# Storing ready-made quarters of the second-level factors from SBUF later, group by group, in a Strassen-Winograd attention-MoE kernel

## The chip, the cores and the metric

The kernel runs on one core of a Trainium2 chip. The metric is the device time of one execution in microseconds (us). A core has engines that run side by side, each with its own queue of instructions: PE (matrix products; its weight loads are listed as PEld), DVE (elementwise), ACT (activations and copies), POOL and SP. In this kernel POOL and SP do little but issue transfers (DMA) between the DRAM of the chip and SBUF, the memory on the core. An instruction waits for others by semaphores, and whatever stands behind it on its queue waits too. Results of PE land in banks of PSUM, which DVE or ACT must read before PE writes them again.

## The reference

A linear attention with decay, block by block, feeds a layer with a hidden size of 2048:

```python
for b in range(nb):                       # blocks of 64 positions
    intra = einsum('bhic,bhjc->bhij', qb, kb) * Dmask
    intra = einsum('bhij,bhjd->bhid', intra, vb)
    inter = einsum('bhid,bhde->bhie', qb * lam_pow, kv_state)
    out[:, :, sl] = intra + inter
    kv_state = lam_block * kv_state + einsum('bhsd,bhse->bhde', kb * rev_pow, vb)
x = out.transpose(0, 2, 1, 3).reshape(B * S, H * D)   # (3072, 512)
h = x @ w_in                                          # (512, 2048)
g = h - np.tanh(h)
return g @ w_out                                      # (2048, 512)
```

The inputs are q, k, v of shape (4, 8, 768, 64), float32; lam of shape (8,); w_in and w_out.

## The kernel before, in words

The 3072 tokens are done in six groups of 512 (128 positions of each of four batches), numbered 0 to 5. A group is: attention, the input product x @ w_in, the nonlinearity, the output product g @ w_out. The loop over groups is staggered: while PE does the output product of one group, the attention and input product of the next are woven in (`attention`, `inner_steps`, `in_turn`), in an order written out by hand.

Both large products are done by Strassen-Winograd, with 7 products of half size in place of 8; from the second group on some of the seven are split once more in the same way. That second level covers products 5 and 6 of the output product from group 1, 4 from group 2, 7 and 3 from group 3 (`twice`). The weight side of such a product needs sums of weight blocks, here called factors:

- `factors`, in DRAM, holds the seven first-level factors of w_out, each 128 rows by 8 blocks (kt) by 256. `sums_out(kt)` (L263) makes one block with four subtractions on DVE and stores it by three transfers on POOL's queue (L272 to L274).
- `fine`, in DRAM, holds the second-level factors: for each of the five products in `TWICE` = (3, 5, 6, 4, 7) seven pieces x of 256 KB, in the order `SUB`. Of a first-level factor cut in quarters b11, b12, b21, b22, three pieces are quarters as they are (x = 1, 2, 3 are b11, b21, b22), and four are sums (x = 5, 7, 6, 4).

The three plain quarters are stored in the first group: `sums_out` has behind its own stores a loop that copies for even kt the first, for odd kt the second and third kind of quarter of all five products into `fine`, in two transfers each (L278 with 64 KB, L279 with 256 KB, in rows of 512 bytes). Over the eight blocks these are 24 transfers and 3.93 MB, issued between 76.6 and 138.3 us.

The four sums are made later, product by product in the order `MADE` = (5, 6, 4, 7, 3). `load_quarters(t)` (L759) loads the four quarters of the t-th of these from `factors` into SBUF by four POOL transfers of 256 KB (L769). `factors_twice(t)` (L772) makes four subtractions on DVE (L781), in the order x = 5, 7, 6, 4, and stores each at once (L782). For t = 0 and 1 the four results go to tiles of their own. For t = 2, 3, 4 they are written in place, into the loaded quarters, which lie in a free part of the hidden tokens' tile (shown as gS): x = 5 goes over b11, 7 over b12, 6 over b22, 4 over b21. The loads of t = 0 and 1 come just ahead of group 1's loop and their sums within it (`make_factors`); the loads of t = 2 come late in group 1 and those of t = 3 late in group 2; their sums stand among the steps of `in_turn`, which also holds the loads and the sums of t = 4, in group 2.

POOL's queue also carries the stream of weight pieces: `piece` keeps eight tiles `wb` of 256 KB filled ahead of PE, from `fine_in` (L792), `fine` (L795) or `factors` (L798); a load waits until PE has read the tile's last content. Also on POOL: stores of results (L815) and, in group 0, raw weights (L216), which SP loads too. SP loads q, k and v: `load_natural` (L138; k_nat, v_nat) and `load_blocks` (L151; 16 transfers for each q_blk and k_blk).

Near the sums of t = 3 stand on DVE L864 and L866, which add product 7 of group 2 (PSUM tile `plain`, in bank z) into two results; `inner_steps` has the matmuls of the next group's input product (L697), some of which write into that bank afterwards. Raw weights are rounded in `round_block` (ACT L291 and following, DVE L296); transposes of q_blk and k_blk are L335, decays of k_nat L404 on ACT, the nonlinearity L600 (ACT) and L601 (DVE).

Of the kernel before, what the change touches and what calls it, by code (L numbers as in the profile page):

```python
# [24 lines left out]
def kernel(  # L25
# [32 lines left out]
    nc = tc.nc  # L58
# [66 lines left out]
    def tied(yes, op):  # L125
        return tc.keep_in_program_order(op) if yes else op
# [67 lines left out]
    SUB = (1, 2, 6, 5, 7, 3, 4)  # L194
    GI = 2
    TWICE = (3, 5, 6, 4, 7)
    fine = dram.tile([len(TWICE), len(SUB), 128, NU, 128], F32, name="fine")
# [65 lines left out]
    def sums_out(kt):  # L263
        bt, tt = pair[kt]
        b11, b12, b21, b22 = (bt[:, x] for x in range(4))
        t1, t2, t4, t3 = (tt[:, x] for x in range(4))
        nc.vector.tensor_tensor(t1, b12, b11, op=AL.subtract)
        nc.vector.tensor_tensor(t2, b22, t1, op=AL.subtract)
        nc.vector.tensor_tensor(t3, b22, b12, op=AL.subtract)
        nc.vector.tensor_tensor(t4, b21, t2, op=AL.subtract)  # L270
        f = factors[:].rearrange("x p k c -> p x k c")
        nc.gpsimd.dma_start(out=f[:, 0:1, kt, :], in_=bt[:, 0:1, :])  # L272
        nc.gpsimd.dma_start(out=f[:, 1:3, kt, :], in_=bt[:, 2:4, :])
        nc.gpsimd.dma_start(out=f[:, 3:NX, kt, :], in_=tt[:, 0:4, :])  # L274

        for x, j in ((1, 0),) if kt % 2 == 0 else ((2, 0), (3, 1)):
            dst = fine[:, SUB.index(x), :, kt // 2, :].rearrange("n p c -> p n c")
            nc.gpsimd.dma_start(out=dst[:, 0:1], in_=bt[:, 3:4, ts(j, 128)])  # L278
            nc.gpsimd.dma_start(out=dst[:, 1:5], in_=tt[:, 0:4, ts(j, 128)])  # L279

    def round_block(w, raw64, first):

# [470 lines left out]
    MADE = (5, 6, 4, 7, 3)  # L753
    quarters = {}
# [4 lines left out]
    def load_quarters(t):  # L759

        for i in range(2):
            for j in range(2):
                if t == 0:
                    x = late["pool"].tile([128, NU, 128], F32, name="wq", tag="wb", bufs=RING)
                elif t > 1:
                    x = hidden(GI + (t > 2), "S1")[:, 2 * i + j].rearrange("p m (v c) -> p (m v) c", v=2)
                else:
                    x = opool.tile([128, NU, 128], F32, name="oq", tag="o")
                tied(t > 1, nc.gpsimd.dma_start(out=x, in_=quarter_source(t, i, j)))  # L769
                quarters[t, i, j] = x  # L770

    def factors_twice(t):  # L772

        b11, b12, b21, b22 = (quarters.pop((t, i, j)) for i in range(2) for j in range(2))
        if t > 1:
            t1, t3, t4, t2 = b11, b12, b21, b22
        else:
            t1, t2, t3, t4 = (late["pool"].tile([128, NU, 128], F32, name=f"wt{x}", tag="sums", bufs=4)
                              for x in (1, 2, 3, 4))
        for x, dst, a, b in ((5, t1, b12, b11), (7, t3, b22, b12), (6, t2, b22, t1), (4, t4, b21, t2)):  # L780
            tc.keep_in_program_order(nc.vector.tensor_tensor(dst, a, b, op=AL.subtract))  # L781
            nc.gpsimd.dma_start(out=fine[TWICE.index(MADE[t]), SUB.index(x)], in_=dst)  # L782
            yield
# [324 lines left out]
    def make_factors(step):  # L1108
        t = TURNS.get(step)
        if t is not None:  # L1110
            if t not in making:
                making[t] = factors_twice(t)
            next(making[t])

# [4 lines left out]
    for g in range(1, NG):  # L1119
        last = g == NG - 1  # L1120
        (p0, p1), step = ahead, 0
        for u in range(NU):
            if u == 0:
                load(g * B + B + 1 if g + 1 < NG else 0)
                kd = decays(g + 1, (0, 1))
            if g < GI:
                for n in (2, 6, 5, 7, 1, 4, 3):
                    if n != 1:
                        up(g, u, n)
                    elif u + 1 < NU:  # L1130
                        up(g, u + 1, 1)
                    else:
                        every(down(g, 1))
                    if u == 0 and n == 5:
                        sums_in(3)
                    step += 1
                    make_factors(step)
                    some(kd, u > 0)
                inner_weights(u, (2, 4, 1))
                if u == 2:  # L1140
                    every(kd)
                if u > 1:
                    run(p0[u - 2:2 * u - 3])
                continue
            if u == 0:
                first = down(g, 1)
                next(first)
                seeded(g, 0, 6)
            if u + 1 < NU:
                seeded(g, u + 1, 6)  # L1150
            for n in (7, 1, 3) if u == 0 else (7, 3, 1) if u + 1 < NU else (7, 3):
                if n == 1:
                    next(first)
                else:
                    seeded(g, u, n)
                some(kd, 2)
            seeded_sums(g, u)
        if g >= GI:
            run(p0[1:3])
        if twice(g, 4):  # L1160
            sums_twice(g, 4)
        every(down(g, 2))
        run(p0[3:4])
        sums_twice(g, 5)
        zw = ("w", "z") if g >= GI else ("z", "w")
        p4 = down_twice(g, 4, zw[0]) if twice(g, 4) else down(g, 4)
        next(p4)
        run(p0[4:])
        every(p4)
        if g < GI:  # L1170
            run(p1[0:1])
        every(kd)
        kd = decays(g + 1, (2, 3))
        if g < GI:
            for u in (0, 1):
                inner_weights(u, (5,))
        sums_once(g, 21, 21, 11)
        sums_twice(g, 6)
        for i, _ in enumerate(down_twice(g, 5, zw[1])):
            some(kd, 2)  # L1180
            if g >= GI and i == 1:
                run(p1[0:1])
        every(kd)
        run(p1[1:3])
        if g < GI:
            for u in (2, 3):
                inner_weights(u, (5,))
            load_quarters(2)
        if twice(g, 7):
            sums_twice(g, 7)  # L1190
        every(down_twice(g, 6, zw[0]))
        if twice(g, 3):
            sums_twice(g, 3)
        run(p1[3:4])
        p7 = down_twice(g, 7, zw[1]) if twice(g, 7) else down(g, 7)
        next(p7)
        run(p1[4:])
        if g == GI:
            load_quarters(3)
        if g < GI:  # L1200
            for u in (0, 1):
                inner_weights(u, (6,))
        every(p7)
        if last:
            down_end(g)
            continue
        if g < GI:
            for u in (2, 3):
                inner_weights(u, (6,))
        ahead = attention(g + 2) if g + 2 < NG else ([], [])  # L1210
        early_pieces = [(att_transpose, g + 2, (0,)), (att_transpose, g + 2, (1,))] if g + 2 < NG else []
        inner_tokens(g + 1, (1,))
        p3 = down_twice(g, 3, "w") if twice(g, 3) else down(g, 3)
        parts = {"down": p3}
        for kind, x in in_turn(g):
            if (kind, x) == (5, 1):
                inner_tokens(g + 1, (5, 2))
                every(parts[1])
                every(p3)
            if (kind, x) == (4, 1):  # L1220
                inner_tokens(g + 1, (4, 6))
                every(parts[5])
                every(parts[2])
                if g >= GI:
                    run(early_pieces)
            if kind not in parts:
                parts[kind] = inner_steps(g + 1, kind)
            next(parts[kind])
            if kind == 1 and x in ((6, 3) if g >= GI else (3,)):
                run(early_pieces[:1])  # L1230
                early_pieces = early_pieces[1:]
            if g < GI and (kind, x) == (4, 5):
                every(factors_twice(2))
            if g == GI and (kind, x) == (1, 5):
                every(factors_twice(3))
            if g == GI and (kind, x) == (5, 6):
                load_quarters(4)
            if g == GI and (kind, x) == (6, 7):
                every(factors_twice(4))
            if kind == 6 and x in (5, 6, 2, 7):  # L1240
                seeded(g + 1, (5, 6, 2, 7).index(x), 11)
                if g < GI and x == 6:
                    run(early_pieces)
        for p in parts.values():
            every(p)
# [30 lines left out]
```

## Time and profile before

| | us |
|---|---|
| median of three runs | 649.3 (646.28, 649.30, 653.39) |
| the profiled execution | 649.38 |
| its span | 647.6 |
| PE busy in the span | 635.9 |
| DVE busy | 477.6 |
| ACT busy | 267.3 |
| POOL busy | 228.6 |
| landing of a wb load from fine, median | 4.0 |
| landing of a quarter (gS from factors), median | 7.5 |

The profile is of one execution. Its parts are: busy time of each engine; the span in 40 equal slices, each digit the busy share in tenths; DMA queues; the chain of work that ended last; groups of instructions by line; DMA issues with the time from issue to landing. In a timeline a row has the start, the duration, the engine, the line, what is written from what, the count, and in brackets how long the engine was idle before it and what released it. The granted clock of PE is at full speed in all slices.

### The profile page before, as it was taken

How to read it: one execution, taken by the hardware profiler on the slowest of the kernel's cores; microseconds unless marked ns; L12 is line 12 of the kernel's file. 1: busy time of each engine (PE TensorE's matmuls, PEld its weight loads, DVE VectorE, ACT ScalarE, POOL GpSimd, SP SyncE). 2: the span in 40 equal slices, each digit the busy share in tenths (PEclk: the TensorE clock that was granted, in tenths of full speed). 3: DMA queues.
4: the chain of work that ended last, by engine and by line, in shares of the span. 5: the costliest groups of instructions: out<-in, count | busy, mean ns of one | idle time of the engine just before them, and what ended most of it. 6: DMA issues, size and time to landing. Idle time of an engine off the chain costs nothing.

```text
span 647.6 us, 16635 instructions
## 1 busy us (share of the span) xinstructions
PE 635.9 (98%) x6440; PEld 584.0 (90%) x6440; DVE 477.6 (74%) x948; ACT 267.3 (41%) x620; POOL 228.6 (35%) x397
## 2 busy tenths in 40 slices
PE   8899999999999999999999999999999999999998
PEld 7788888888888899998999998999998899998997
DVE  4468697785898867569967569988667987467953
ACT  4789676503432422345331247333245332334310
POOL 0000255735443454410455431355321254520161
PEclk9999999999999999999999999999999999999999
DMA  9979998969765999775889986798884577832484
GB/s 215 219 192 245 315 273 278 346 191 266 207 167 124 294 264 303 210 191 121 211 242 289 289 211 160 173 280 242 261 182 96 134 237 241 246 104 76 102 287 150
DMA packets 166190, 139.80 MB, mean 216 GB/s; under 512 B 136864, under 2 KB 138016, under 8 KB 166112
## 3 DMA queue, kind: packets, MB, share of 16 engines
q0 software_dynamic: 31792, 104.62, 51.1%
q1 hardware_dynamic: 134176, 34.12, 26.2%
q8 instruction: 51, 0.84, 0.6%
q14 instruction: 27, 0.22, 0.1%
q10 hardware_dynamic: 144, 0.00, 0.0%
HBM read 111.94 MB, written 26.74 MB: 214 GB/s over the span
## 4 chain that ended last, share of the span: by engine, by line
PE 46%; issue 19%; DMA 10%; DVE 8%; POOL 8%; SPq 6%; ACT 3%; POOLq 0%; DVEq 0%; ACTq 0%
PE acc L994 7%; PE h L965 6%; DMA q_blk<-in_q_dram 5%; PE y L906 5%; SPq L151 4%; PE plain L849 4%; PE y L554 4%; POOL wb L795 4%; PE zw L906 3%; PE y L697 3%; PE z L554 2%; POOL wb L792 2%; DMA k_blk<-in_k_dram 2%; DMA k_nat<-in_k_dram 1%; PE z L697 1%
## 5 line engine op out<-in xcount | busy, mean ns | idle before, releaser
L795 POOL DMA_DIRECT2D wb<-fine x133 | 71.7, 540 | 159.2 <-PE plain L849 108.8
L849 PE MATMUL plain<-wb,g 128*128 128x256 f32 x416 | 96.0, 381 | 0.0
L849 PEld LDWEIGHTS plain<-wb,g 128*128 128x128 f32 x416 | 77.5, 190 | 10.4
L965 PE MATMUL h<-xt,w 128*128 128x256 f32 x256 | 58.3, 382 | 1.4 <-DVE w L296 1.4
L798 POOL DMA_DIRECT2D wb<-factors x64 | 34.5, 540 | 71.2 <-PE z L697 47.9
L910 ACT ACTIVATE q<-y 128x128 f32<-128x128 f32 x76 | 21.1, 278 | 87.4 <-PE y L906 86.3
L965 PEld LDWEIGHTS h<-xt,w 128*128 128x128 f32 x256 | 47.5, 190 | 8.7 <-DVE w L296 1.8
L906 PE MATMUL y<-wb,g 128*128 128x128 f32 x336 | 44.8, 278 | 0.0
L792 POOL DMA_DIRECT2D wb<-fine_in x60 | 32.5, 544 | 28.8 <-PE z L697 10.8
L600 ACT ACTIVATE th<-g 128x512 f32<-128x512 f32 x48 | 29.4, 627 | 29.8 <-DVE g L625 29.6
L906 PEld LDWEIGHTS y<-wb,g 128*128 128x128 f32 x336 | 40.7, 192 | 0.7
L688 ACT ACTIVATE g<-y 128x512 f32<-128x512 f32 x24 | 14.3, 597 | 63.1 <-PE y L697 63.1
L404 ACT ACTIVATE k_nat<-k_nat,mask 128x64 f32<-128x64 f32 (+1 forms) x128 | 35.0, 335 | 1.7 <-DMA k_nat<-in_k_dram 1.7
L994 PE MATMUL acc<-wt,g 128*128 128x256 f32 x144 | 32.9, 380 | 0.2 <-DVE g L973 0.2
L601 DVE TENSOR_TENSOR g<-g,th 128x512 f32<-128x512 f32 x48 | 32.1, 683 | 0.4
L697 PE MATMUL z<-tt,wb 128*128 128x128 f32 x256 | 31.9, 275 | 0.0
L994 PEld LDWEIGHTS acc<-wt,g 128*128 128x128 f32 x144 | 27.2, 190 | 4.3 <-DVE g L973 0.6
L906 PE MATMUL zw<-wb,g 128*128 128x128 f32 x224 | 30.2, 278 | 0.1
L619 PE MATMUL y<-xt,w 128*128 128x256 f32 x128 | 30.3, 379 | 0.0
L619 PE MATMUL zs<-xt,ws 128*128 128x256 f32 x128 | 30.2, 379 | 0.0
L697 PEld LDWEIGHTS z<-tt,wb 128*128 128x128 f32 x256 | 30.2, 192 | 0.0
L292 ACT ACTIVATE r<-raw 128x512 int16<-128x512 uint32 x32 | 25.2, 787 | 8.8 <-DMA raw<-in_moe_w_out_dram 4.6
(236 smaller groups left out, 1475.0 us busy)
## 6 DMA issues: line engine op xcount, KB each, us to landing
wb<-fine POOLq DMA_DIRECT2D x133, 256.0 KB, 4.0
wb<-factors POOLq DMA_DIRECT2D x64, 256.0 KB, 4.3
wb<-fine_in POOLq DMA_DIRECT2D x60, 256.0 KB, 4.8
v_nat<-in_v_dram SPq DMA_DIRECT2D x24, 256.0 KB, 5.2
raw<-in_moe_w_out_dram POOLq DMA_DIRECT2D x12, 512.0 KB, 6.0
k_nat<-in_k_dram SPq DMA_DIRECT2D x20, 256.0 KB, 4.9
fine<-wt POOLq DMA_DIRECT2D x17, 256.0 KB, 3.5
raw<-in_moe_w_in_dram SPq DMA_DIRECT2D x8, 512.0 KB, 5.0
```

The source lines that it names most:

```text
L404: tc.keep_in_program_order(nc.scalar.activation(k_h, k_h, AF.Copy, scale=mask[0:rows, h % 2, h // 2, HALF - 1:HALF]))
L554: nc.tensor.matmul(out=t[:, m, :], lhsT=wt[:, kt, ts(m, 128)], rhs=x[:, kt, :], start=first and m == 0 and kt == 0, stop=kt == 1, skip_gro ...
L601: nc.vector.tensor_tensor(dst(c), src, th, op=AL.subtract)
L619: nc.tensor.matmul(out=t[:, m, :], lhsT=wt[:, kt, ts(m, 128)], rhs=x[:, kt, :], start=False, stop=kt == 1, skip_group_check=True)
L697: nc.tensor.matmul(out=dst[:, ts(u, 128)], lhsT=a, rhs=b, start=(x in (1, 5) or x == 2 and not filled) and u == 0, stop=True, skip_group_c ...
L792: nc.gpsimd.dma_start(out=t.rearrange("p m c -> p (m c)"), in_=fine_in[INNER.index(n_[1]), (5, 6, 3).index(x_)].rearrange("p u c -> p (u c)"))
L795: nc.gpsimd.dma_start(out=t.rearrange("p m c -> p (m c)"), in_=fine[TWICE.index(n_), SUB.index(x_)].rearrange("p u c -> p (u c)"))
L798: nc.gpsimd.dma_start(out=t, in_=factors[XAT[FACT[n_][1]]][:, 2 * x_:2 * x_ + 2, :])
L849: tied(held["yes"], nc.tensor.matmul(out=t[:, m, :], lhsT=a[:, u, kt, ts(m, 128)], rhs=wb[:, kt, :], start=first and u == 0 and m == 0 and ...
L906: tied(held["yes"], nc.tensor.matmul(out=dst, lhsT=a[:, u, :], rhs=wb[:, ts(u, 128)], start=x in (1, 2) and u == 0, stop=u == NU - 1, skip ...
L965: tied(u == 0 or held["yes"], nc.tensor.matmul(out=hm[c][:, m, :], lhsT=w1[u][:, i, a, ts(m, 128)], rhs=xt[0, t][:, i, :], start=m == 0 an ...
L994: tied(held["yes"], nc.tensor.matmul(out=acc[n][:, r, :], lhsT=a[:, ts(r, 128)], rhs=b, start=kt == 0 and r == 0, stop=kt == KH - 1, skip_ ...
```

## The change

The loop at the end of `sums_out` goes. A new function, `quarters_alone(t)`, stores the three plain quarters of the t-th product straight from the tiles that `load_quarters(t)` has filled: three POOL transfers of 256 KB with rows of 2 KB. It is called ahead of the first sum of t = 0 and of t = 1 in `make_factors`; at the end of the output product of groups 1 and 2 for t = 2 and 3; and among the steps of group 2 for t = 4. In all 15 transfers with the same 3.93 MB. Loads and sums stay as they are. As the sums of t = 2, 3, 4 are written into the loaded quarters, the sums that overwrite b11, b22 and b21 now come after the stores of these have landed. In the changed kernel the lines behind the removed loop have numbers lower by 5, those behind the new function by 1.

```diff
@@ sums_out
         nc.gpsimd.dma_start(out=f[:, 3:NX, kt, :], in_=tt[:, 0:4, :])
-
-        for x, j in ((1, 0),) if kt % 2 == 0 else ((2, 0), (3, 1)):
-            dst = fine[:, SUB.index(x), :, kt // 2, :].rearrange("n p c -> p n c")
-            nc.gpsimd.dma_start(out=dst[:, 0:1], in_=bt[:, 3:4, ts(j, 128)])
-            nc.gpsimd.dma_start(out=dst[:, 1:5], in_=tt[:, 0:4, ts(j, 128)])
@@ behind load_quarters
+    def quarters_alone(t):
+        for x, i, j in ((1, 0, 0), (2, 1, 0), (3, 1, 1)):
+            nc.gpsimd.dma_start(out=fine[TWICE.index(MADE[t]), SUB.index(x)], in_=quarters[t, i, j])
@@ make_factors
             if t not in making:
+                quarters_alone(t)
                 making[t] = factors_twice(t)
@@ the loop over groups
         if last:
             down_end(g)
             continue
+        if g in (1, GI):
+            quarters_alone(1 + g)
         if g < GI:
@@ the steps of in_turn
+            if g == GI and (kind, x) == (4, 2):
+                quarters_alone(4)
             if g == GI and (kind, x) == (6, 7):
                 every(factors_twice(4))
```

## The prediction

> **What bounds the kernel now.** I read the page first: its engine rows and its slices.
>
> ```profile
> PE 635.9 (98%) x6440; PEld 584.0 (90%) x6440; DVE 477.6 (74%) x948; ACT 267.3 (41%) x620; POOL 228.6 (35%) x397
> PE   8899999999999999999999999999999999999998
> POOL 0000255735443454410455431355321254520161
> DMA  9979998969765999775889986798884577832484
> ```
>
> PE is busy for 635.9 of 647.6 us, so all its gaps together are 11.7 us. POOL, on whose queue the edit acts, is busy for a third of the span. The third row that matters is DMA: its engines are full (9) in many slices, also from 340 to 372 us. Then I asked for busy time by stretch, to see where the 11.7 us lie:
>
> ```profile
> 0.00:99.00 99.00, 92.31 (x1056) 79.02 (x1056) 65.61 (x137) 71.88 (x135) 15.06 (x29) 1.00 0.98 246
> 99.00:144.20 45.20, 45.20 (x217) 39.81 (x210) 34.63 (x74) 18.75 (x31) 24.87 (x39) 1.00 0.85 275
> ...
> 345.00:384.00 39.00, 39.00 (x317) 38.08 (x316) 26.92 (x54) 11.57 (x20) 19.17 (x33) 1.00 0.90 255
> ```
>
> The columns are the stretch, its length, the busy time of PE, PEld, DVE, ACT, POOL, the granted clock, the DMA share and GB/s. 6.7 us of gaps lie before 99 us, 4.0 after 552 (the tail); from 99 to 552 us only 1.0 is left. A kernel so bound by PE gains from an edit on POOL only what a PE gap holds, but loses whatever makes PE wait. Third, what the removed stores cost on POOL, from the groups by line within 75 to 144 us:
>
> ```profile
> L279 POOL DMA_DIRECT2D fine<-wt x9 | 6.8, 755 | 0.9 <-issue 0.9
> L278 POOL DMA_DIRECT2D fine<-wt x9 | 5.0, 554 | 0.0
> L279 POOL DMA_DIRECT2D fine<-ws x3 | 2.3, 754 | 0.2 <-issue 0.2
> L278 POOL DMA_DIRECT2D fine<-ws x3 | 1.7, 557 | 0.0
> ```
>
> Last, the timelines of POOL, DVE and PE around each place where stores come in. The one without room is that of MADE[3] (product 7) in the third group; three timelines in turn:
>
> ```profile
> 337.05 2.98 POOL L769 DMA_DIRECT2D gS<-factors  x4
> 341.47 0.55 POOL L798 DMA_DIRECT2D wb<-factors  x1 [1.44 <-DMA wb<-factors]
> ```
>
> ```profile
> 345.47 0.69 DVE L781 TENSOR_TENSOR gS<-gS 128x512 f32<-128x512 f32 x1 [1.34 <-DMA gS<-factors]
> ...
> 347.49 0.69 DVE L781 TENSOR_TENSOR gS<-gS 128x512 f32<-128x512 f32 x1 [1.12 <-DMA gS<-factors]
> ...
> 348.30 0.68 DVE L781 TENSOR_TENSOR gS<-gS 128x512 f32<-128x512 f32 x1
> 348.90 0.68 DVE L864 TENSOR_TENSOR q<-q,plain 128x512 f32<-128x512 f32 x1
> 349.50 0.68 DVE L866 TENSOR_TENSOR q<-q,plain 128x512 f32<-128x512 f32 x1
> ```
>
> ```profile
> 351.48 1.06 PE L697 MATMUL w<-xt,w 128*128 128x128 f32 x8
> ```
>
> DVE already waits here for the quarters' loads (1.34 and 1.12 us). Right behind the third subtraction (L781) stand L864 and L866, the last readers of PSUM bank z; in the built program the matmuls at 351.48 wait for exactly L866. It ends at 350.18, so the slack is 1.30 us.
>
> **The change part by part.** The sum is made against the profiled execution, 649.38 us (span 647.6 and 1.78 around it); that is 0.08 above the median of 649.3, so both readings are the same. Only POOL's order of instructions changes in the built program; PE, DVE, ACT and SP keep theirs.
>
> *Removed from group 0.* 12 stores of L278 by 0.55 and 12 of L279 by 0.75 us make 6.7 + 9.1 = 15.8 us of POOL's time and 3.93 MB, between 76.6 and 138.3 us. In 99–144.2 PE has no gap (45.20 of 45.20); in 75–99 it has two, 0.18 and 0.88 us, and those wait for DVE and ACT, not for a transfer. Gain: 0. L994's matmuls run there at 0.216 us each, as L554's do elsewhere, so less traffic does not make them faster. What can move is the SP queue. Its q_blk loads start at 130.63, right after the last rounding of weights (L296, 130.56). That stands behind ACT's L291, which waited 0.97 us for raw weights at 125.58 and could otherwise start only when PE's last matmul of its block ends, at 125.89. So SP starts 0 to 1 us earlier.
>
> *Added for MADE[0] and [1], 144–163.* Their 8 loads are issued 144.73–152.85; the 6 stores, 4.5 us of issue at most by the 0.75 of a load, follow as the loads land (5.4 and 6.9 us). The wb loads at 152.85–156.24 move back by some 5 us. Their first use is at 189.24, and POOL then sits idle 6.92 us until 163.16, where it waits for DVE. These factors go to tiles of their own, so no subtraction waits for a store. Cost 0; cover: 27 us of prefetch. Without that cover it would be 5 us.
>
> *Added for MADE[2], 238–244.* The 3 stores put the wb loads of 241.58 and 243.30 back by up to 2 us; PE uses them at 252.49 and 253.38, about 7 us after they land. Its subtractions (in place, like those of [3]) come at 257.50, over 8 us after the stores' issue; a store from the same tiles took 4.4 us in 248–262. Cost 0; with landings of 7.8 us the cover would just be gone.
>
> *Added for MADE[4], 366–371.* Loads 363.08–366.05, stores behind them, subtractions not before 380.82: 10 us of room. Cost 0.
>
> *Added for MADE[3], 344–352.* POOL's new order is: four loads (337.05–340.03); a store waiting for the first load; one wb; the stores waiting for the third and the fourth load; two wb. The subtractions write into the loaded tiles, so they now wait for the stores as well: the first for store 1, the third for store 3, the fourth for store 2. Store 3 cannot be issued before its quarter landed, 347.45 by DVE's own wait in the timeline. How long a store of 256 KB takes is the unknown. The same form (fine<-gS) had a median of 4.5 us in 346–364, 4.4 in 248–262 and 6.6 in 372–386; the row of L782 over the whole run goes from 2.6 to 7.4, that of the removed L279 from 2.9 to 7.8. I take 4.5, the same place: 347.5 + 4.5 = 352.0. Behind that stand the third subtraction, L864 and L866, spaced 0.60, and 0.68 for the last: 352.0 + 0.60 + 0.60 + 0.68 = 353.9. PE wants it at 351.48: **stall 2.4 us**. In short, landing time less 2.1: at 2.6 us of landing 0.5, at 7.8 it is 5.7; loads that land 1 us earlier (less SP traffic) take 1 off. The first subtraction, by store 1 (issued about 344.9, landing 349.4), is done in time for that. Behind the stall, the wb loads that the two stores put back from 342.48 and 344.08 to about 348.1 and 348.7 land at the 5.3 us of this window at about 353.4 and 354; PE wants them at 354.99 and 355.89, plus the stall: hidden, by 1.6 us if there is none. DVE then has some 3 us of arrears. Its next waits on PE are 2.19 us at 362.28 and 1.17 at 364.14, and nothing between is nearer to PE than L714 (about 1.6 us), which is late by no more than PE itself. So the stall is neither recovered nor multiplied.
>
> *Rule weighed.* Row: 4.5 us for such a store. The Trainium skill, DMA: Bandwidth & Descriptors, section Anatomy of one DMA — SWDGE (gpsimd) path, gives a transfer as about 2.0 us plus its bytes at 436 GB/s, an estimate of 2.6 us here, and hence a stall of 0.5. The trace disagrees: with DMA at 9 tenths, 4.5 was measured.
>
> Sum: 0 + 0 + 0 + 0 + 2.4 = +2.4, so 649.38 + 2.4 = **651.8 us**.
>
> **The rivals.**
> 1. *Hidden after all.* Stores land at the fast end (2.6 to 3.1 us), or PE's real slack is larger because its ends in a profile are modelled. Stall 0 to 1, time 649.4 to 650.4. For it: stores whose last bytes meet emptier queues; against: DVE's two waits for loads of 7.6 and 8.2 us in the same stretch say that the queues are full.
> 2. *Faster.* SP's stream, continuous from 130.63 to about 290, starts up to 1 us earlier. It brings k_nat at 288.90, for which ACT (L404) waited 1.73 and then DVE (L601) 3.10; from there DVE runs almost without a gap to PE's gaps of 0.59 at 304.21 and 0.10 at 319.25. If the earlier start holds, those 0.7 go: time 648.7 if the stall is hidden as well. It decides only if the stall is under 0.7. Against: between lie 0.77 MB of new stores in 232–260, where DMA is full.
> 3. *SP late.* The same chain the other way: those 0.77 MB, at the 264 to 303 GB/s moved there, are 2.8 us of a full DMA. The part that SP bears, 1 to 2.8 us, delays k_nat, and L601's chain to PE has 0 slack: 651.8 + 1 to 2.8 = 652.8 to 654.6. The Trainium skill, DMA: Bandwidth & Descriptors, section Issuing engines are not separate DMA queues, says that transfers of all queues share the same 16 engines. The trace shows that here in SP's 16 q_blk loads, which took between 7.7 and 12.8 us. Against: SP was relieved of as many bytes before.
> 4. *Slow store.* Landing of 6.6 to 7.8: stall 4.5 to 5.7, time 653.9 to 655.1.
>
> **How the numbers follow.** Stall of 1 to 4 us: 0.50 (650.4 to 653.4). Rival 1: 0.22. Rival 2: 0.08. Rival 3: 0.10. Rival 4: 0.10. The likeliest gives 651.8. The range leaves out what is beyond the ends of rivals 2 and 4 and adds about 1 us for what runs of one kernel differ (646.28 to 653.39 before): 647.5 to 656. One per cent, about what a measurement of this kernel can tell from no change, is 6.5 us. Faster by that would need over half of all PE gaps: 0.03. Slower needs a store of over 8.6 us, or rivals 3 and 4 together: 0.09. Within: 0.88.
>
> **What would show it.** In the new profile: L278 and L279 gone and PE still gapless in 99–144; a PE wait at L697 of about 2.4 us for DVE L866 near 351–354; DVE's third subtraction there (L780 in the new numbering) waiting for DMA fine<-gS until about 352; no new PE wait at 189, 252–258 and 381; PE's gaps at 304 and 319 as before within 1 us. Wrong if the wait at 351 is absent or over 4.5 us, if PE waits for wb anywhere, or if the gaps at 304 to 319 have grown.

## The result, and the profile after

The changed kernel takes 650.5 us (median of 20 runs, 648.9 to 655.73); the kernel before, run beside it, 647.51 (20 runs, 645.66 to 653.39). The ratio is 1.0044, with a 95% interval of 1.0027 to 1.0061: slower by 2.85 us (1.7 to 4.0), within 1%. A second measurement, with 12 runs, gave 1.0052 (1.0034 to 1.0071). The forecast of +2.4 us came out in sign and size, but for half the reason: there are two costs in place of one. The forecast one was smaller in most profiles than forecast, the other was not seen, and that the two errors nearly cancel is luck.

One thing must be known before the traces are laid side by side. The profiled execution after took 648.99 us, the one before 649.38. The first is at the fast end of its kernel's runs, the second 1.9 us above its own median. So spans are of no use here; places are. PE's order of instructions is the same in both, and so the start of the same matmul in both can be compared, stretch by stretch.

The engine rows of the page after, and two of its slices:

```profile
PE 636.8 (98%) x6440; PEld 583.8 (90%) x6440; DVE 477.5 (74%) x948; ACT 267.7 (41%) x620; POOL 221.9 (34%) x388
POOL 0000233427443455410455631354320244521261
DMA  9979987749866889884899995698883467732394
```

POOL has nine transfers less (397 to 388 instructions) and is busy 6.7 us less; its digits are lower in the sixth to ninth slice (81 to 146 us), and DMA's as well. Next the stretches, with the columns that the prediction explains:

```profile
99.00:144.20 45.20, 45.20 (x211) 39.80 (x210) 35.19 (x76) 17.90 (x28) 15.19 (x23) 1.00 0.63 200
144.20:215.00 70.80, 70.15 (x558) 60.22 (x557) 54.21 (x121) 23.05 (x54) 34.17 (x55) 1.00 0.79 224
...
345.00:384.00 39.00, 38.26 (x313) 37.30 (x312) 26.85 (x54) 11.57 (x20) 22.84 (x40) 1.00 0.99 293
```

Where the stores went, DMA is down from 0.85 to 0.63 and POOL from 24.87 to 15.19 us, and PE is without a gap as it was: that relief buys nothing. Where they came in, PE has two new gaps, 0.65 us in the second row and 0.74 in the third. Three lines of PE's waits name them:

```profile
PE w L692 <- DVE q L865: 0.7, 1, 0.7
...
PE z L549 <- DVE g L575: 0.5, 1, 0.5
...
PE y L549 <- ACT g L567: 0.2, 1, 0.2
```

**The third group.** DVE, PE and POOL in turn, around the sums of product 7:

```profile
346.86 0.69 DVE L780 TENSOR_TENSOR gS<-gS 128x512 f32<-128x512 f32 x1 [3.81 <-DMA fine<-gS]
...
349.26 0.69 DVE L780 TENSOR_TENSOR gS<-gS 128x512 f32<-128x512 f32 x1 [0.70 <-DMA fine<-gS]
349.87 0.68 DVE L863 TENSOR_TENSOR q<-q,plain 128x512 f32<-128x512 f32 x1
350.47 0.68 DVE L865 TENSOR_TENSOR q<-q,plain 128x512 f32<-128x512 f32 x1
```

```profile
351.30 1.13 PE L692 MATMUL w<-xt,w 128*128 128x128 f32 x8 [0.74 <-DVE q L865]
```

```profile
335.77 2.98 POOL L764 DMA_DIRECT2D gS<-factors  x4
...
345.67 0.55 POOL L769 DMA_DIRECT2D fine<-gS  x1 [0.27 <-issue]
```

The chain is as forecast: the third subtraction waits for the store of b22, L863 and L865 stand behind it, and PE waits for L865. Only the sizes are smaller. The quarters landed after 7.0 us (7.8 before), the store took 3.5.

**The first steps of group 1.** Here the prediction had no cost. POOL, DVE and PE after:

```profile
153.76 0.54 POOL L769 DMA_DIRECT2D fine<-wq  x1 [0.20 <-issue]
155.08 0.54 POOL L769 DMA_DIRECT2D fine<-oq  x1 [0.77 <-DMA oq<-factors]
157.01 0.54 POOL L769 DMA_DIRECT2D fine<-oq  x1 [1.39 <-DMA oq<-factors]
158.09 0.54 POOL L769 DMA_DIRECT2D fine<-oq  x1 [0.55 <-DMA oq<-factors]
158.63 2.14 POOL L797 DMA_DIRECT2D wb<-factors  x4
...
164.17 1.53 POOL L648 DMA_DIRECT2D fine_in<-ws  x2 [1.20 <-DVE ws L645]
```

```profile
169.16 0.69 DVE L780 TENSOR_TENSOR wt<-wq 128x512 f32<-128x512 f32 x1 [4.00 <-DMA fine_in<-ws]
...
172.18 0.68 DVE L575 TENSOR_TENSOR g<-g,z 128x512 f32<-128x512 f32 x1
```

```profile
172.91 1.99 PE L549 MATMUL z<-tt,ws 128*128 128x256 f32 x8 [0.48 <-DVE g L575]
```

Before, POOL sent the transfers of `inner_weights` (fine_in<-ws, sums for the input product) at nearly the same time, and DVE waited half as long for them:

```profile
164.22 1.56 POOL L653 DMA_DIRECT2D fine_in<-ws  x2
...
168.47 0.69 DVE L781 TENSOR_TENSOR wt<-wq 128x512 f32<-128x512 f32 x1 [2.05 <-DMA fine_in<-ws]
```

Four wb loads of 1 MB together leave POOL at 158.6 to 160.8 in place of 152.9 to 156.2, and so less time lies between them and fine_in<-ws (164.17). The DMA row of a view of 162 to 168 us (40 slices of 0.15 us), before and after, shows the engines nearly idle at first in the one and full in the other:

```profile
DMA  1430000001440309899660459977259378999999
...
DMA  5998987987889989998899998999989999799899
```

In this view the fine_in<-ws land after a median of 4.6 us, 4.0 before. DVE's delay is more than these 0.6 us: in the profile after POOL also stood idle for 1.20 us ahead of the first of them (the row at 164.17), though DVE had the data of the first ready at 162.5. The wait does not hang on that pause: in undo_third, below, POOL does not pause there, the median is 6.0 us, and DVE waits 4.05 us all the same. The sum of product 5 on DVE waits for this landing (4.00 us, before 2.05); its result tile comes from the same four buffers ("sums") as the tile under transfer, which inplace, below, puts to the test. Behind it on DVE's queue stands L575, and PE waits for that.

### The profile page after: what moved, and what is told of

The parts are those of the page before. It is cut to its first block, busy times and chain, and to the rows that moved or that the text cites. A ratio compares the mean times of both kernels' runs of the same rounds, so it can differ in the third digit from the quotient of the medians.

```text
span 647.2 us, 16614 instructions
## 1 busy us (share of the span) xinstructions
PE 636.8 (98%) x6440; PEld 583.8 (90%) x6440; DVE 477.5 (74%) x948; ACT 267.7 (41%) x620; POOL 221.9 (34%) x388
## 4 chain that ended last, share of the span: by engine, by line
PE 82%; DMA 6%; DVE 3%; SPq 3%; issue 2%; ACT 2%; POOL 1%; DVEq 0%; POOLq 0%; ACTq 0%
PE plain L848 12%; PE y L692 11%; PE y L905 10%; PE zw L905 7%; PE h L964 7%; PE z L692 5%; PE y L614 4%; PE zs L614 4%; PE acc L993 4%; SPq L151 3%; PE w L692 3%; DMA k_nat<-in_k_dram 2%; PE y L549 2%; PE op L496 2%; PE op L477 1%
## 5 line engine op out<-in xcount | busy, mean ns | idle before, releaser
L272 POOL DMA_DIRECT2D factors<-wt x6 | 3.5, 575 | 72.4 <-DVE wt L291 72.2
```

## The experiments

Theory A is the prediction's: the loss is the wait in the third group. Theory B came from the profile after: the larger part is lost in the first steps of group 1. The table holds, for each kernel, what PE loses in two stretches against the first profile of before (start of the same matmul ahead of and behind the stretch), its waits for wb<-fine near the end, and the ratio to the kernel before (12 runs each; 11 of double, 6 of wait_known). The ratios were taken in three sets, each with its own runs of the kernel before: the changed kernel again to double, before_again to moved, and inplace to wait_known. In the rows "before; again" and "changed; again" the ratio is that of the second measurement.

| kernel | 172–190 us | 345–360 us | waits at 615–632 | ratio, 95% interval |
|---|---|---|---|---|
| before; again | 0; 0 | 0; 0 | 0.9; 0.5 | 0.9998 (0.9976–1.0020) |
| changed; again | 1.2; 2.1 | 1.0; 3.9 | 0; 0 | 1.0052 (1.0034–1.0071) |
| undo_first | 0 | 0.3 | 1.3 | 0.9999 (0.9979–1.0020) |
| undo_third | 1.2 | 0 | 1.0 | 1.0010 (0.9997–1.0023) |
| double | 2.0 | 0.8 | 0 | 1.0047 (1.0022–1.0073) |
| late_third | 2.1 | 0 | 0 | 0.9995 (0.9977–1.0013) |
| late_first | 2.1 | 2.1 | 0 | 1.0017 (1.0001–1.0032) |
| moved | 2.5 | 0 | 0 | 0.9997 (0.9981–1.0013) |
| inplace | 0 | 1.3 | 0 | 1.0027 (1.0004–1.0050) |
| mixed | 0 | 0 | 0 | 0.9999 (0.9987–1.0010) |
| both_places | 0 | 0 | 0 | 0.9996 (0.9981–1.0010) |
| wait_known | 0 | 4.2 | 0.2 | 1.0039 (1.0025–1.0054) |

The runs of one kernel spread over some 1 to 8 us, so the ratios carry 0.7 to 1.7 us each way; the places of waits are the sharper evidence, though each is of one execution.

**The changed kernel again** (no edit).

> The changed kernel once more, for a second profile and a second ratio. Theory A (the cost is the wait in the third group, PE 351 us): ratio to before about 1.004, PE waits at the matmuls behind L865 for 0.7 us or more. Theory B (the cost is mostly in the first steps of group 1, where weight loads pushed behind the new stores make the transfers of the input product's factors land late): again a PE wait of 0.5 us or more for DVE near 173 us, and one of 0.2 near 175. If the gaps at 304 and 319 us are gone again, the earlier start of SP's loads is a real gain and not chance.

Both waits are back, larger: 1.4 us at 174 and 1.95 at 353. The gaps at 304 and 319 are gone again; before_again, below, says what that is worth. What is new stands behind the second. PE's rows, and then stretches of 1 us, where the granted clock is the third number from the right, ahead of DMA share and GB/s:

```profile
353.10 1.13 PE L692 MATMUL w<-xt,w 128*128 128x128 f32 x8 [1.95 <-DVE q L865]
354.07 3.20 PE L848 MATMUL plain<-wb,g 128*128 128x256 f32 x8
```

```profile
354.00:355.00 1.00, 1.00 (x7) 0.86 (x6) 1.00 (x3) 0.00 (x0) 1.00 (x3) 0.74 0.91 289
355.00:356.00 1.00, 1.00 (x4) 0.82 (x3) 1.00 (x5) 0.00 (x0) 1.00 (x3) 0.50 1.03 300
356.00:357.00 1.00, 1.00 (x3) 0.79 (x3) 1.00 (x6) 0.00 (x0) 1.00 (x2) 0.50 0.94 187
357.00:358.00 1.00, 1.00 (x6) 0.94 (x5) 0.96 (x3) 0.00 (x0) 1.00 (x3) 0.55 0.97 331
```

Eight matmuls that take 1.89 us elsewhere take 3.20 (the next eight 1.46 in place of 1.05): the clock of PE was halved for 2 x (0.26 + 0.50 + 0.50 + 0.45) = 3.4 us, which costs 1.7 us on top of the wait. The Trainium skill, TensorE: Matmul & The Clock Gate, Part 1 (the HAM clock gate), has such a halving in windows of 3.4 us, after PE was idle for one window or more. The length agrees; the condition does not, since here a wait of 1.95 us was enough.

**undo_first**: the first two products as before.

```diff
+        for x, j in ((1, 0),) if kt % 2 == 0 else ((2, 0), (3, 1)):
+            dst = fine[:, SUB.index(x), :, kt // 2, :].rearrange("n p c -> p n c")
+            nc.gpsimd.dma_start(out=dst[:, 1:3], in_=tt[:, 0:2, ts(j, 128)])
...
-                quarters_alone(t)
```

> Products 5 and 6 (the first two that are made) get their plain quarters in the first group again; the rest stays as changed. Theory A: time as the changed kernel, ratio about 1.004. Theory B: the waits near 173 and 175 us go, 1.1 us or more are won back, ratio 1.001 to 1.0025.

The waits at 173 and 175 are gone, as theory B had it; the time came back to that of before, more than expected. The third group lost only 0.3 us in this profile, which still has its stores.

**undo_third**: product 7 as before (the same loop with `dst[:, 4:5]` and `tt[:, 3:4]`), `quarters_alone(3)` left out.

> Only product 7 (made in the third group at 340 to 352 us) gets its plain quarters in the first group again. Theory A: the wait for L865 goes and with it the whole loss, ratio 0.999 to 1.001. Theory B: only about 0.7 us are won back, ratio about 1.003, and the waits near 173 us stay.

The wait for L865 is gone, the ones at 173 stay. About 0.4% is won where theory B allowed 0.1%. With the 0.5% of undo_first that is nearly twice what the change costs, so the ratios, at 0.1 to 0.2% each way, do not divide the loss between the places. That both take part is said by the profiles: theory A alone cannot have the waits at 173, theory B alone not the one at 351.

**double**: the old stores and the new ones.

> The old stores in the first group and the new ones as well, so that nothing is removed; the pieces are stored twice with the same content. If the removal by itself gains nothing (theory A's first term, 0), the ratio is that of the changed kernel, about 1.004, and the gaps at 304 and 319 us are the same in both. If the removal brings SP's loads forward and so wins about 1 us, the ratio is about 1.006 and the two gaps are back.

The ratio is that of the changed kernel. So the additions alone make the loss, and the removal gains nothing that could be measured; at 0.25% each way a gain of 1 us would not show. The two are not quite alike either: here POOL pauses for 2.26 us at 318.5, and PE waits 0.92 us for wb<-fine at 326, which no profile of the changed kernel has.

**before_again** (no edit).

> The kernel before once more, for a second profile. If the earlier start of SP's loads is no effect of the change, PE's gap of 0.6 us at 304 (and the one of 0.1 at 319) will be gone here too; if it is one, they stay. No PE wait at 173 and 351 us by both theories. Ratio 0.998 to 1.002.

The 0.6 us at 304 are gone without any change, and most of the 0.1 at 319: chance of one execution, and no gain of an earlier SP stream. In wait_known, below, which keeps the order of transfers of before, the gap at 304 is there again (0.98 us). The wait near the end is again there (0.5).

**late_third**: the sums of product 7 one step later.

```diff
-            if g == GI and (kind, x) == (1, 5):
+            if g == GI and (kind, x) == (1, 6):
                 every(factors_twice(3))
```

> The changed kernel with the four sums of product 7 one step later, so that L863 and L865, the readers of bank z, come before the second to fourth sum on DVE's queue. If the store of b22 stalls PE only through this queue, the wait at 351 us and every drop of the granted clock behind it go, the waits at 173 stay: ratio 1.001 to 1.003, like the undone third group. If PE is late for another reason (weights behind the stores), ratio 1.004 to 1.005.

No wait at 351. L863 and L865 now come before the second sum; DVE still waits 1.72 us for the first store, and no matmul waits for that. The waits at 173 stay (1.4 and 0.2). The ratio is below what was expected: PE loses 2.1 us in the profile, and the time is that of the kernel before (see moved).

**late_first**: the plain quarters of products 5 and 6 behind the four sums of each.

```diff
...
-                quarters_alone(t)
                 making[t] = factors_twice(t)
             next(making[t])
+            if TURNS.get(step + 1) != t:
+                quarters_alone(t)
```

The lines left out keep the loaded tiles for these later stores, and hold the stores at their place in the program.

> The changed kernel with the plain quarters of products 5 and 6 stored behind the four sums of each instead of ahead of the first. Theory B: the weight loads are no longer pushed into the way of the first transfers of the input product's factors, the waits at 173 and 175 us go, the one at 351 stays: ratio 1.002 to 1.004. If it is the mere number of bytes about that time that counts, the waits at 173 stay or move by some us: about 1.005.

The loss is not gone, it has moved by one step of the loop:

```profile
185.73 1.99 PE L549 MATMUL z<-tt,ws 128*128 128x256 f32 x8 [1.17 <-DVE g L575]
188.13 1.99 PE L549 MATMUL y<-xt,w 128*128 128x256 f32 x8 [0.41 <-ACT g L567]
```

Now the three stores of product 5 (169.6 to 171.2) are in the way of the next sums for the input product; those of product 6 leave only at 185.3. A wb load waits 3.08 us for one of these stores, since the quarters of product 5 lie in tiles of the wb ring; it and the two behind it leave at 174.3 to 176.5 (before: 170.6 to 172.9), right ahead of fine_in<-ws at 176.98. A sum of product 6 on DVE then waits 4.57 us for fine_in<-ws (before: 0.41). So wb loads are pushed here too, and the chain is that of 173: what the run refutes is only that storing ahead of the first sum, and not behind the fourth, does the harm. The ratio, 1.0017, is below both expectations, though PE loses 4.2 us in the profile.

**moved**: both moves.

> Both moves together: stores later for products 5 and 6, sums later for product 7. If the two places are the whole loss, the time is that of the kernel before, ratio 0.999 to 1.001. If the removal from the first group is a gain by itself, 0.997 to 0.999. If more is lost elsewhere, above 1.001.

The profile has the 1.5 us at 187 and none at 351, and the ratio is 1. Against its own row in the table that is 1.6 to 2 us too fast: 2.5 us are lost and 0.5 to 0.9 of waiting saved near the end. The same holds for late_third and late_first of this set. The kernel before was slower in it (median 649.02, in the others 647.2 to 647.5; each set ran on another chip). Against those other medians late_third (648.77), moved (648.52) and late_first (650.08) would be 1 to 3 us slower, late_first most. That fits better, but it compares runs of different sets and is no proof.

**inplace**: all sums in the loaded quarters.

```diff
-        if t > 1:
+        if True:
             t1, t3, t4, t2 = b11, b12, b21, b22
```

> The changed kernel with the sums of products 5 and 6 also made in place, in the loaded quarters, so that they take no tile that a transfer of the input product's factors still reads. The stores and their bytes stay as changed. If that shared tile is the way by which the new stores delay DVE and so PE at 173 us, the wait there goes (1.2 to 2.1 us won), the one at 351 stays: ratio 1.001 to 1.004. If PE waits there for another reason, the wait stays and the ratio is 1.004 to 1.006.

Stores and bytes as in the changed kernel, no wait at 173 or 175; the one at 351 stays with 1.1 us. DVE's sums wait for no fine_in<-ws any more, although POOL sends these later, between the stores of the sums (from 165.4 us). This shows the way of the loss: it goes through the shared buffers, and the bytes alone, which are the same, do not make PE wait.

**mixed**: undo_first with the move of late_third.

> Products 5 and 6 get their plain quarters in the first group as before, and the sums of product 7 come one step later: neither of the two places is left. If they are the whole loss and the removal gains nothing, ratio 0.999 to 1.001. If the shorter POOL queue gains by itself (the wait of 0.5 to 0.9 us near 621 us that both profiles of the kernel before show and the changed one does not), 0.997 to 0.999.

**both_places**: inplace with the move of late_third.

> All stores as changed, sums of products 5 and 6 in place and those of product 7 one step later. If each of the two waits is what its mend says, none is left: ratio 0.998 to 1.000, and the best of the versions with the change. If the transfers themselves cost time, 1.001 to 1.003.

Both are free of the two waits and have the time of the kernel before (647.37 and 647.21 against 647.35). No version beats it by more than the uncertainty.

**wait_known**: a PE wait of known length in the kernel before, with nothing else changed.

```diff
-            nc.vector.tensor_tensor(o, res[g, 5], t, op=AL.add)
+            for _ in range(4 if g == GI else 1):
+                nc.vector.tensor_tensor(o, res[g, 5], t, op=AL.add)
```

> The kernel before, where the last reader of bank z in the third group (L866 there) is done four times in place of once with the same result; by the rows of before the last one ends at 353.8 us in place of 350.2, a wait of 2.4 us for PE at 351.5 that has nothing to do with transfers. If a wait costs its length: ratio 1.0035 to 1.004, clock 1.0. If a wait of this length often halves the granted clock for one stretch of 3.4 us behind it, as in one profile of the changed kernel, up to 1.7 us come on top: 1.004 to 1.0065, and the mean clock of many runs is 0.997.

```profile
352.50 1.13 PE L697 MATMUL w<-xt,w 128*128 128x128 f32 x8 [2.26 <-DVE q L867]
353.47 3.27 PE L849 MATMUL plain<-wb,g 128*128 128x256 f32 x8
```

The wait is 2.26 us, and again eight matmuls need 3.27 us behind it, at a granted clock of 0.50 from 354 to 357 us. Of six runs three had a mean clock of 1.0 (649.02 to 649.84 us) and three of 0.997 (650.98 to 651.48): 2.1 us between the medians, where 1.7 was worked out. Only one of the three was profiled; that the other two have the same cause is inferred. For it speaks that the kernel before, which has no such wait, has 14 of 98 runs at 0.997 in the three sets, and their medians lie within 0.7 us of the others'.

## Why the prediction was right, and where it was wrong

- *Removal, "Gain: 0".* Right as far as it can be measured: no PE gap in 99–144 before or after, and double costs what the change costs. Rival 2 (SP earlier) loses its gain by before_again, where the gap at 304 is gone without the change. Of rival 3 (SP late) there is no sign: after 298 us the gaps did not grow in any profile of the changed kernel. Its figures of 7.7 and 12.8 us are those of two rows of 16 k_blk loads; the rows of q_blk go from 8.1 to 11.8.
- *MADE[0] and [1], "no subtraction waits for a store. Cost 0; cover: 27 us of prefetch".* This step failed, and the forecast size came out in spite of it. It followed the wb loads only to their own reader. The subtraction waits for a store of another kind, fine_in<-ws, through the buffers that both share, and DVE's 2.05 us of idle time in front of it were already in the profile of before. It measured 1.2 to 2.1 us; undo_first and inplace take it away.
- *MADE[2] and [4], "Cost 0".* Right: PE's matmuls keep their distance in 232–298 and 360–436 us in all profiles, to 0.01 us.
- *MADE[3], "stall 2.4 us".* Mechanism right, by undo_third and late_third. The size was too large: PE lost 1.0, 2.2 (without the slow clock), 2.1, 1.3, 0.8 and 0.3 us there in six profiles (changed, again, late_first, inplace, double, undo_first). So it lies between rival 1 (0 to 1) and the forecast, nearer the one or the other from run to run. The term mis-sized is the time of quarters and store: in the changed kernel's two profiles 7.0 and 6.9 us for the quarters in place of 7.8, and 3.5 and 4.8 for the store in place of 4.5. The estimate of 2.6 us from the Trainium skill (DMA: Bandwidth & Descriptors, Anatomy of one DMA — SWDGE (gpsimd) path), which the prediction weighed, was too low for both. Rival 4 (a store of 6.6 us or more) did not come in them.
- *Not in the sum: the clock.* A wait of some 2 us here can cost 1.7 more. After one of 1.95 and one of 2.26 us it did, after one of 1.88 it did not. A mean clock of 0.997 is not proof of it, since late_third and inplace show the same mean without this, from a phase of half clock in their first 20 us.
- *Not in the sum: the end.* Both profiles of before have POOL standing still for 2.8 us there, though its buffers come free every 0.9 us, and then a burst (here of the first):

```profile
612.32 0.54 POOL L795 DMA_DIRECT2D wb<-fine  x1 [0.35 <-PE y L906]
615.65 2.78 POOL L795 DMA_DIRECT2D wb<-fine  x5 [2.79 <-PE y L906]
```

PE then waits 0.9 (again: 0.5) us for wb<-fine. In the kernels with 388 POOL instructions this pause is not at that place and the wait is missing; with 394 and 397 in undo_first and undo_third the burst comes at 622 and 626. The pause alone is not enough: mixed, with 394, has it at the same transfer as undo_first, and PE does not wait. What makes POOL pause, I did not find; the row's releaser is only inferred. The number of instructions does not place it either, since before and undo_third have 397 each and pause 12 transfers apart. So a gain at the end is seen in profiles only, and that the change makes it is not shown.
- *The sum.* By the table the changed kernel loses 1.2 + 1.0 us in its first profile and 2.1 + 3.9 in its second, with 1.7 of slow clock; less 0.5 to 0.9 at the end that is 1.3 to 1.7 and 5.1 to 5.5. The 2.85 measured lie between, and no closer sum can be made from two profiles. The forecast time was 1.3 us too high since the profiled execution that it stood on was 1.9 above the median of 20 runs, and the change 0.5 too small. Why late_third and moved, which lose 2 us and more in their profiles, measure like the kernel before is not settled. That the two waits together make the loss is shown by both_places, which has all the stores as changed, neither wait, and the time of before; what share each has is not.

## What to carry to other kernels

When a transfer is put back, follow not only who reads its data but what lies behind it in the queues, and who holds a buffer until that has landed: idle time that a profile already shows in front of an instruction, with a DMA as its end, marks such a place. A wait holds up the queue of the engine that does the waiting, so short instructions that free a PSUM bank belong ahead of it. Where two profiles are to be compared in an order that is the same, compare places, not spans, and take a second profile of the kernel before ahead of any story on a gap of half a microsecond.

## What the runs showed of the hardware

Two things were unexpected. Behind a PE wait of 1.95 us (the changed kernel again) and one of 2.26 us (wait_known), both in full work, the granted clock was halved for 3.4 us; behind one of 1.88 us (late_first) it was not. In wait_known the runs with the lower mean clock are 2.1 us slower than the others, where the halved clock by itself comes to 1.7. And POOL's queue stood still for 2.8 us at one place of the program, at the same transfer in two profiles of the kernel before and at others in undo_first and undo_third.
